# Loading the first weights of a mixer kernel in joint quarters of Wq and Wk, ahead of the transposing DMA

## The chip, the cores and the metric

The kernel runs on one core of one Trainium2 chip. TensorE (PE) multiplies matrices into PSUM, which has 8 banks of 128 x 512 float32; VectorE (DVE) and ScalarE (ACT) do the element-wise work, GpSimd (POOL) a few memsets, SyncE (SP) issues DMAs, and so can ACT. Each engine runs its own instructions in the order written and waits for others at semaphores. The metric is the device time of one execution in microseconds, as the median of several runs.

## The reference

One input x of 2048 rows (S) and 512 columns (D), in bfloat16, goes through two branches that a gate mixes:

```python
qkv = x @ wqkv                       # 512 -> 3 x 512, 32 heads of 16
# A: each position attends to 8 positions: itself and 2, 4, ... 14 back
logits = einsum(q, kg) * scale; attn = softmax(logits)
a = einsum(attn, vg) @ wo
# B: layernorm over D, then an MLP over the 2048 positions
u = gelu(w1.T @ layernorm(x) + b1)   # 1792 x 512
b = w2.T @ u + b2                    # 2048 x 512
g = sigmoid(sum(x * gate_w, -1))
out = g * a + (1 - g) * b
```

## The kernel before

Everything lives in one block of SBUF (`arena`). x is held twice: as rows (X, 16 tiles of 128 x 512, for layernorm and the MLP) and transposed (XT, four blocks of 128 columns of D by 2048 positions, for the projections). PE's work in order is:

1. seven warm-up matmuls on a constant (L536, written into bank 7), with four small ones (L544) between them that transpose a part of x,
2. the projections (L617) of Q and K, then V. An output group `dl` of 128 takes every fourth column of a weight, so four groups make 512, and each group has four matmuls, one for each quarter `dt` of the 512 rows of the weight; four blocks `sb` of 512 positions,
3. two bursts of 64 small matmuls (L696) that sum DVE's products of Q and shifted K (L688) over the head's 16 elements,
4. the MLP's first matmul (L810), its second (L860), and the attention's output projection (L876).

ACT evicts the projections from PSUM into Q5 (L625), K5 and V5 (L628); K5 has a pad of zeros in front, set by a POOL memset (L420). DVE computes the statistics of layernorm (L572), the products of Q and K (L688), softmax, the products with V (L795, L798), and at the end the mix (L897).

The order on each engine is found while the program is built. Each operation is given a duration, reads and writes, and a list scheduler (`_Sched`) places it at the earliest possible time; loads at the start have a landing time written by hand (`lands`), with the waits for earlier loads cleared. For DVE most of the order is written out by hand (`chain`): the statistics of tiles 0 to 3 come before the first product of Q and K, which reads Q and K of blocks 0 and 1. The bursts L696 have a high priority and go in where their products are planned to be ready. On the chip each engine keeps the planned order, whatever the real times.

The start concerns us. x's block 0 (positions 0 to 511) is transposed in two ways. Its columns 0 to 127 are loaded plainly by ACT's queue (`d_xp`, into XP), transposed by the four matmuls L544 and evicted by ACT (L553) and DVE (L555). Its columns 128 to 511 come by one transposing DMA on SP's queue (`ld_xt0`, L473, called xt0 here). Wq comes in four quarters of 128 KB: the first on ACT's queue behind the plain columns, the others on SP's behind xt0. Wk follows in two halves of 256 KB, then rows of x (`x0`: tiles 0 and 1), then the transposing DMA for block 1 (`xt1`, L460), x2, x4 (tiles 4 to 7), xt2, xt3 and the rest. L429 issues the plain DMAs.

PE's first projections (block 0) go over eight banks: Q's four groups in banks 0 to 3, K's four in banks 4 to 7. Banks 0 to 3 take quarter 0 in turn, then quarters 1, 2 and 3; then banks 4 to 7 take quarters 0 and 1, and then 2 and 3. From block 1 on, groups take all four quarters at once and rotate over banks 0 to 3, so each waits for the eviction of the group four before it:

```python
first = [(tn, dl) for tn in range(2) for dl in range(4)]
for (b0, d0, d1, s0, s1) in ((0, 0, 1, 0, 512), (0, 1, 2, 0, 512), (0, 2, 3, 0, 512),
                             (0, 3, 4, 0, 512), (4, 0, 2, 0, 512), (4, 2, 4, 0, 512)):
    for b in range(b0, b0 + 4):
```

Of the kernel before, what the change touches and what calls it, by code (L numbers as in the profile page):

```python
# [13 lines left out]
D = 512  # L14
# [6 lines left out]
PAD = 14  # L21
SC = 512
KROW = S + 32
# [310 lines left out]
def bass_gated_mix__sliding_local_dilated__mixer_token_mlp__prompt_kernel(nc, A_x, A_wqkv, A_wo, B_x, B_w1, B_b1, B_w2, B_b2, gate_w, out, dbg=None):  # L334
    with contextlib.ExitStack() as es:
# [3 lines left out]
        sch = _Sched()  # L339
# [3 lines left out]
        wqkv_v = A_wqkv.rearrange("(dt p) c -> p dt c", p=128)  # L343
# [7 lines left out]
        WQKV = view("WQKV", BF16, [(3 * D, 4), (1, 3 * D)])  # L351
# [10 lines left out]
        K5 = view("K5", BF16, [(KROW, 4), (1, KROW)])  # L362
# [45 lines left out]
        def sub(ap_, offs, dims):  # L408
            return bass.AP(ap_.tensor, ap_.offset + offs, [list(ap_.ap[0])] + [list(d) for d in dims])

        def psub(ap_, p0, np_, offs, dims):
# [3 lines left out]
        A = sch.add  # L415
# [1 line left out]
        c_ident = A("pool", lambda e: e.affine_select(out=IDENT, in_=nc.const_aps.tensor(1.0, [128, 128], BF16), pattern=[[1, 128]], compare_op=ALU.is_equal,  # L417
                                                     fill=0.0, base=0, channel_multiplier=-1),
                    0.4, writes=["ident"], name="ident")
        A("pool", lambda e: e.memset(sub(K5, 0, [(KROW, 4), (1, PAD)]), 0.0), 0.2, writes=["k5pad"], name="k5pad")  # L420
        A("pool", lambda e: e.memset(sub(V5, 0, [(KROW, 4), (1, PAD)]), 0.0), 0.2, writes=["v5pad"], name="v5pad")
        def f_rp(e):
            with nc.allow_low_precision(reason="exact 0/1 indicator sums"):
# [4 lines left out]
        def mk_dma(dst, src):  # L428
            return lambda e: e.dma_start(dst, src)  # L429

        init_dmas = []

        def throttle():
            return [init_dmas[-5]] if len(init_dmas) >= 5 else []

        def prev_dma():
            return [init_dmas[-1]] if init_dmas else []

        def ld_x(t0, n, q="sp"):
            ds = sch.dsem("x%d" % t0)  # L440
            op = sch.dma(q, mk_dma(X[:, t0:t0 + n, :], xv[:, t0:t0 + n, :]), n * 128 * D * 2, ds,
                         writes=["x%d" % t for t in range(t0, t0 + n)], deps=throttle() if q == "sp" else [], after=prev_dma() if q == "sp" else [], name="d_x%d" % t0)
            if q == "sp":
                init_dmas.append(op)
            return op

        def ld_w(tn, d0, n, q="sp"):
            ds = sch.dsem("wqkv%d_%d" % (tn, d0))
            op = sch.dma(q, mk_dma(WQKV[:, d0:d0 + n, tn * D:(tn + 1) * D], wqkv_v[:, d0:d0 + n, tn * D:(tn + 1) * D]),
                         n * 128 * D * 2, ds, writes=["wqkv%d_%d" % (tn, dt) for dt in range(d0, d0 + n)],  # L450
                         deps=throttle() if q == "sp" and n == 4 else [], after=prev_dma() if q == "sp" else [],
                         issue=0.65 if n == 4 else 0.45, name="d_wp%d_%d" % (tn, d0))
            if q == "sp":
                init_dmas.append(op)
            return op

        def ld_xt(sb):
            ds = sch.dsem("xt%d" % sb)
            dst = XT[:, :, sb * 512:(sb + 1) * 512]
            op = sch.dma("sp", lambda e: e.dma_start_transpose(dst, x2d[sb * 512:(sb + 1) * 512, :]), 512 * D * 2, ds,  # L460
                         writes=["xt_%d" % t for t in range(4 * sb, 4 * sb + 4)], deps=throttle(), after=prev_dma(), name="d_xt%d" % sb)
            init_dmas.append(op)
# [4 lines left out]
        def xt_of(sb, d0=0, d1=4):  # L467
            return XT0[d0:d1] + (XT0[4:] if d0 == 0 else []) if sb == 0 else ["xt_%d" % t for t in range(4 * sb, 4 * sb + 4)]

        def ld_xt0():  # L470
            ds = sch.dsem("xt0")
            dst = XT[:, 1:4, 0:512]
            op = sch.dma("sp", lambda e: e.dma_start_transpose(dst, x2d[0:512, 128:512]), 512 * 384 * 2, ds, issue=1.25,  # L473
                         writes=XT0[1:4], after=prev_dma(), name="d_xt0")
            init_dmas.append(op)
            return op

        XP = view("OUTS", BF16, [(128, 4), (1, 128)])
        d_xp = sch.dma("act", mk_dma(XP, xv[:, 0:4, 0:128]), 512 * 128 * 2, sch.dsem("xp"), writes=["outs0"], issue=0.4, name="d_xp")

        first_loads = [ld_w(0, 0, 1, "act"), ld_xt0(), ld_w(0, 1, 1), ld_w(0, 2, 1), ld_w(0, 3, 1), ld_w(1, 0, 2), ld_w(1, 2, 2),
                       ld_x(0, 2)]
        ld_xt(1)
        first_loads.append(init_dmas[-1])
        for op_, t_ in zip(first_loads, (3.4, 4.6, 5.0, 5.4, 5.8, 6.6, 7.4, 8.2, 10.6)):
            op_.lands = t_
            op_.deps.clear()
        d_xp.lands = 3.1
        first_loads[0].order.add(d_xp)
        init_dmas[:] = [first_loads[1]] + first_loads[5:]  # L490
        ld_x(2, 2)
        ld_x(4, 4)
        ld_xt(2)
# [6 lines left out]
        def ld_w1(j):  # L500
# [4 lines left out]
            if j < 4:  # L505
# [8 lines left out]
                       writes=["wo"], deps=throttle(), after=prev_dma(), name="d_wo")  # L514
# [4 lines left out]
        for i_, (v_, n_) in enumerate(((B_b1, NFT), (B_b2, NST))):  # L519
            vr = v_.rearrange("(t q j) -> q t j", q=4, j=32)  # L520
            for q_ in range(4):
                sch.dma("sp", mk_dma(psub(BR, 32 * q_, n_, 32 * i_, [(1, 32)]), vr[q_]), n_ * 64, ds_b, reads=["br"],
                        writes=["br_%d_%d" % (i_, q_)], deps=throttle(), after=prev_dma(), name="d_b_%d_%d" % (i_, q_), issue=0.45)
        d_w1.append(ld_w1(3))
        A("dve", lambda e: e.transpose(out=BT, in_=BR), 0.2, reads=["br_%d_%d" % (i_, q_) for i_ in range(2) for q_ in range(4)],
          writes=["btc"], name="t_b")
# [5 lines left out]
        def f_warm(n, w_=D):  # L532
            def fn(e):
                ins = None
                for _ in range(n):
                    ins = e.matmul(ps[:, 7, 0:w_], lhsT=CONE[:, 0:128], rhs=CONE[:, 0:w_], start=True, stop=True)  # L536
                return ins
            return fn

        def f_tr(h):  # L540
            def fn(e):
                ins = None
                for t in range(2):
                    ins = e.matmul(ps[:, 5 + h, 128 * t:128 * t + 128], lhsT=XP[:, 2 * h + t, :], rhs=IDENT, start=True, stop=True)  # L544
                return ins
            return fn
# [2 lines left out]
        w2_ = A("pe", f_warm(1, 256), 0.2, writes=["lg7_0", "lg7_1"], name="warm2", prio=-100)  # L549
        ta_ = A("pe", f_tr(0), 0.215, reads=["outs0", "ident"], writes=["lg5_0", "lg5_1"], after=[w2_], name="tr0", prio=-100)  # L550
        tr_ = A("pe", f_tr(1), 0.215, reads=["outs0", "ident"], writes=["lg6_0", "lg6_1"], after=[ta_], name="tr1", prio=-100)
        w3_ = A("pe", f_warm(1), 0.43, writes=["lg7_0", "lg7_1"], after=[tr_], name="warm3", prio=-100)
        A("act", lambda e: e.activation(out=XT[:, 0, 0:256], in_=ps[:, 5, 0:256], func=AF.Copy), 0.35, reads=["lg5_0", "lg5_1"],  # L553
          writes=["xt0_0"], name="ev_tra", prio=0)
        A("dve", lambda e: e.tensor_copy(out=XT[:, 0, 256:512], in_=ps[:, 6, 0:256]), 0.35, reads=["lg6_0", "lg6_1"],  # L555
          writes=["xt0_0b"], name="ev_trb", prio=0)
# [55 lines left out]
        def f_proj(tn, dl, sb, bank, d0=0, d1=4, s0=0, s1=512):  # L612
            def fn(e):
                ins = None
                for dt in range(d0, d1):
                    lhsT = sub(WQKV, dt * 3 * D + tn * D + dl, [(4, 128)])
                    ins = e.matmul(ps[:, bank, s0:s1], lhsT=lhsT, rhs=XT[:, dt, sb * 512 + s0:sb * 512 + s1],  # L617
                                   start=(dt == 0 and s0 == 0), stop=(dt == 3))
                return ins
            return fn  # L620
# [9 lines left out]
        tnames = ["q", "k", "v"]  # L630
        first = [(tn, dl) for tn in range(2) for dl in range(4)]
        fbn = [["acc%d" % b] for b in range(4)] + [["lg%d_0" % b, "lg%d_1" % b] for b in range(4, 8)]
        for (b0, d0, d1, s0, s1) in ((0, 0, 1, 0, 512), (0, 1, 2, 0, 512), (0, 2, 3, 0, 512), (0, 3, 4, 0, 512), (4, 0, 2, 0, 512), (4, 2, 4, 0, 512)):
            for b in range(b0, b0 + 4):
                tn, dl = first[b]
                last_main[0] = A("pe", f_proj(tn, dl, 0, b, d0, d1, s0, s1), 0.216 * (d1 - d0) * (s1 - s0) / 512,
                                 reads=xt_of(0, d0, d1) + ["wqkv%d_%d" % (tn, dt) for dt in range(d0, d1)],
                                 writes=fbn[b], after=[last_main[0]], name="pf_%s%d_%d_%d" % (tnames[tn], dl, d0, s0))
                last_main[0].order.add(w3_)
        for b, (tn, dl) in enumerate(first):  # L640
            A("act", f_evq(tn, dl, 0, b), 0.52, reads=fbn[b] + (["k5pad"] if tn == 1 else []),
              writes=["%s5_%d_0" % (tnames[tn], dl)], name="ev_%s%d_0" % (tnames[tn], dl), prio=0)
# [7 lines left out]
        for (tn, dl, sb) in seq_proj:  # L650
# [4 lines left out]
                             writes=["acc%d" % bank], after=[last_main[0]], name="pj_%s%d_%d" % (tnames[tn], dl, sb), prio=0)  # L655
            A("act", f_evq(tn, dl, sb, bank), 0.62, reads=["acc%d" % bank] + (["k5pad"] if tn == 1 else ["v5pad"] if tn == 2 else []),
              writes=["%s5_%d_%d" % (tnames[tn], dl, sb)], name="ev_%s%d_%d" % (tnames[tn], dl, sb), prio=0)
# [11 lines left out]
                writes=["xa"] + ["wqkv%d_%d" % (tn, dt) for tn in range(3) for dt in range(4)], name="d_xa")  # L669
        for t in range(NST):  # L670
# [5 lines left out]
          writes=["th"], name="g_tanh", prio=0)  # L676
# [31 lines left out]
        for wh in range(2):  # L708
# [6 lines left out]
            for (dl, c0, nc_) in pieces:  # L715
# [5 lines left out]
                  writes=wr, name="qkm_%d_%d_%d" % (wh, dl, c0), prio=0)  # L721
            rd = sum([pbn(b_) for b_ in bufs], []) + PBX[wh] + ["rp"]
            for wl in range(4):
                qop = A("pe", f_qkr(list(enumerate(bufs)), (wl,)), 0.92, reads=rd, writes=["lg%d_0" % (4 + wl), "lg%d_1" % (4 + wl)],
                        name="qkr_%d_%d" % (wh, wl), prio=-100 + wl, delay=BURST_DELAY)
                A("act", (lambda wh_, wl_: (lambda e: e.activation(out=ATT[:, :, 4 * wh_ + wl_, :], in_=ps[:, 4 + wl_, :].rearrange("p (h c) -> p h c", h=2), func=AF.Copy)))(wh, wl),  # L726
                  0.55, reads=["lg%d_0" % (4 + wl), "lg%d_1" % (4 + wl)], writes=["lw%d" % (4 * wh + wl)],
                  name="lev_%d_%d" % (wh, wl), prio=0)
# [60 lines left out]
        for k_, u in enumerate(USEQ):  # L789
# [7 lines left out]
            for (nm, n_, du) in (("ava", 4, 2.25), ("avb", 2, 1.2)):  # L797
                A("dve", (lambda pv_, n__: (lambda e: e.tensor_tensor(out=pv_[:, 0:n__], in0=pv_[:, 0:n__], in1=pv_[:, n__:2 * n__], op=ALU.add)))(pv, n_),  # L798
                  du, writes=[pn], name="%s_%d" % (nm, u))
# [27 lines left out]
        for ft in range(NFT):  # L827
# [6 lines left out]
              name="gel_%d" % ft, prio=0)  # L834
# [84 lines left out]
        for i in range(NST):  # L919
# [4 lines left out]
            elif i > 1:  # L924
# [6 lines left out]
              name="t1_%d" % i, prio=0)  # L931
# [119 lines left out]
```

## Time and profile before

| what | value |
|---|---|
| median of 3 runs | 168.18 us (167.72 to 168.53) |
| the profiled execution's own time | 168.55 us |
| its span | 167.3 us |
| granted PE clock | 1.00 |
| first projection matmul (L617) starts | 5.61 us |
| first product of Q and K (L688) starts | 15.07 us |
| last combine (L897) ends | 165.65 us |

The span goes from the first to the last instruction of one profiled execution; times of single instructions count from its start. The page gives busy time by engine, the chain of work that ended last, and groups of instructions by line of the kernel; further answers of the trace give waits, single stretches of time, and for each DMA the time from its issue to its landing. A line such as `arena<-in_A_x_dram` reads "written tile <- read tensor". "SPq" and "ACTq" are the queues on which SP and ACT issue DMAs.

### The profile page before, as it was taken

Reading aid. Unit: us, or ns where it says so; the run is one execution under the profiler, and the core shown is the slowest. Engines: PE = TensorE matmul, PEld = TensorE weight load, DVE = VectorE, ACT = ScalarE, POOL = GpSimd, SP = SyncE. Lnnn points to the kernel's source line nnn. Section 1 sums busy time; section 2 is a strip of 40 time slices with the busy share of each in tenths; the row PEclk is TensorE's granted clock in tenths of the full one; section 3 lists DMA queues with packets and bytes.
Section 4 is the critical chain, followed back from the end, with each engine's and each line's share of the span. In section 5 each row is a group of like instructions: output and inputs, shape, how many; then the busy total and the mean of one; then the engine's idle time right before and its main releaser. Section 6 shows DMA issues by size and latency. Waiting matters only on the chain.

```text
span 167.3 us, 2136 instructions
## 1 busy us (share of the span) xinstructions
PE 162.1 (97%) x845; PEld 77.5 (46%) x859; DVE 151.3 (90%) x154; ACT 75.1 (45%) x116; POOL 0.7 (0%) x8
## 2 busy tenths in 40 slices
PE   7699999999999999999999999999999999999994
PEld 2355555554454444444444444444444444444463
DVE  1055999999999999999999999999999999999896
ACT  3077688889899818793131121131231321310100
POOL 1000000000000000000000000000000000000000
PEclk9999999999999999999999999999999999999999
DMA  5999999959003846996779926462672570000454
GB/s 135 327 268 216 314 316 290 303 165 308 2 0 97 311 116 179 307 290 155 181 189 340 339 76 142 113 187 71 181 218 83 138 223 0 0 0 0 157 190 159
DMA packets 47625, 29.64 MB, mean 177 GB/s; under 512 B 9856, under 2 KB 46464, under 8 KB 47616
## 3 DMA queue, kind: packets, MB, share of 16 engines
q1 hardware_dynamic: 45120, 24.85, 54.4%
q10 hardware_dynamic: 2496, 4.66, 10.2%
q8 instruction: 7, 0.11, 0.3%
q14 instruction: 2, 0.02, 0.0%
HBM read 21.24 MB, written 2.10 MB: 140 GB/s over the span
## 4 chain that ended last, share of the span: by engine, by line
PE 91%; DMA 3%; DVE 2%; ACT 2%; issue 1%; ACTq 0%
PE ps L860 29%; PE ps L810 29%; PE ps L617 23%; PE ps L876 6%; PE ps L696 4%; DMA arena<-in_A_wqkv_dram 3%; DVE arena L897 2%; ACT L585 1%; ACT arena L628 1%; ACTq L429 0%; ACT arena L585 0%
## 5 line engine op out<-in xcount | busy, mean ns | idle before, releaser
L860 PE MATMUL ps<-arena 128*128 128x512 bf16 x220 | 48.5, 379 | 0.2
L810 PE MATMUL ps<-arena 128*128 128x512 bf16 x219 | 48.2, 379 | 0.4 <-issue 0.2
L617 PE MATMUL ps<-arena 128*128 128x512 bf16 x188 | 41.4, 379 | 1.6 <-DMA arena<-in_A_wqkv_dram 1.3
L688 DVE TENSOR_TENSOR arena<-arena 128x4096 bf16<-128x4096 bf16 (+1 forms) x12 | 35.5, 2998 | 2.5 <-ACT arena L628 2.1
L795 DVE TENSOR_TENSOR arena<-arena 128x8192 bf16<-128x8192 bf16 x8 | 35.0, 4419 | 0.0
L860 PEld LDWEIGHTS ps<-arena 128*128 128x128 bf16 x224 | 21.9, 98 | 26.4
L810 PEld LDWEIGHTS ps<-arena 128*128 128x128 bf16 x224 | 21.8, 98 | 26.6 <-ACT arena L726 0.4
L617 PEld LDWEIGHTS ps<-arena 128*128 128x128 bf16 x192 | 21.6, 113 | 21.5 <-issue 1.8
L928 ACT ACTIVATE arena<-ps,arena 128x512 bf16<-128x512 f32 x16 | 12.5, 778 | 39.4 <-PE ps L860 39.4
L798 DVE TENSOR_TENSOR arena<-arena 128x4096 bf16<-128x4096 bf16 (+1 forms) x16 | 27.0, 1751 | 0.0
L628 ACT ACTIVATE arena<-ps 128x512 bf16<-128x512 f32 x32 | 18.6, 596 | 4.5 <-PE ps L617 4.5
L831 ACT ACTIVATE arena<-ps,arena 128x512 bf16<-128x512 f32 x14 | 9.6, 687 | 22.2 <-PE ps L810 16.6
L572 DVE BATCH_NORM_STATS2 arena<-arena 128x6 f32<-128x512 bf16 x16 | 10.0, 682 | 6.1 <-DMA arena<-in_A_x_dram 6.1
L876 PE MATMUL ps<-arena 128*128 128x512 bf16 (+1 forms) x79 | 14.1, 336 | 0.1
L897 DVE SCALAR_TENSOR_TENSOR arena<-ps,arena 128x512 bf16<-128x512 f32 (+1 forms) x20 | 11.5, 637 | 0.9 <-PE ps L876 0.7
L596 ACT ACTIVATE arena<-arena 128x512 bf16<-128x512 bf16 x16 | 12.2, 804 | 0.0
L625 ACT ACTIVATE arena<-ps 128x512 bf16<-128x512 f32 x16 | 9.0, 597 | 6.2 <-PE ps L617 6.1
L876 PEld LDWEIGHTS ps<-arena 128*128 128x128 bf16 x80 | 7.8, 98 | 6.2
L672 DVE SCALAR_TENSOR_TENSOR arena<-arena 128x512 bf16<-128x512 bf16 x16 | 10.1, 689 | 0.0
L742 DVE TENSOR_TENSOR arena<-arena 128x512 bf16<-128x512 bf16 (+4 forms) x11 | 7.3, 667 | 0.6 <-ACT arena L761 0.2
L696 PE MATMUL ps<-arena 128*32 128x512 bf16 x128 | 7.3, 380 | 0.0
L726 ACT ACTIVATE arena<-ps 128x512 bf16<-128x512 f32 x8 | 4.7, 592 | 4.6 <-PE ps L696 4.6
(42 smaller groups left out, 40.0 us busy)
## 6 DMA issues: line engine op xcount, KB each, us to landing
arena<-in_B_w_dram SPq DMA_DIRECT2D x7, 1024.0 KB, 8.5
arena<-in_B_w_dram SPq DMA_DIRECT2D x8, 896.0 KB, 5.2
arena<-arena ACTq DMA_DIRECT2D x32, 128.0 KB, 2.9
arena<-in_A_x_dram SPq DMA_DIRECT2D x4, 512.0 KB, 6.1
out_dram<-arena SPq DMA_DIRECT2D x14, 128.0 KB, 1.7
arena<-in_A_x_dram SPq DMA_DIRECT2D x1, 1536.0 KB, 7.9
arena<-in_A_wqkv_dram SPq DMA_DIRECT2D x2, 256.0 KB, 3.8
arena<-in_A_x_dram SPq DMA_DIRECT2D x2, 256.0 KB, 3.6
```

The costliest lines, as they stand in the source:

```text
L596: A("act", (lambda t_: (lambda e: e.activation(out=X[:, t_, :], in_=X[:, t_, :], func=AF.Identity, scale=col(RSTD, t_), bias=col(NMR, t_)) ...
L617: ins = e.matmul(ps[:, bank, s0:s1], lhsT=lhsT, rhs=XT[:, dt, sb * 512 + s0:sb * 512 + s1], start=(dt == 0 and s0 == 0), stop=(dt == 3))
L628: return lambda e: e.activation(out=dst, in_=ps[:, bank, :], func=AF.Copy)
L688: return lambda e: e.tensor_tensor(out=PBL[buf][:, :, 512 * c0:512 * (c0 + nc_)], in0=in0, in1=in1, op=ALU.mult)
L696: ins = e.matmul(ps[32 * c:32 * c + 32, 4 + wl, :], lhsT=RP, rhs=PBL[buf][:, wl, c * 512:(c + 1) * 512], start=(dl == 0), stop=(dl == 3), ...
L795: A("dve", (lambda o_, i0, i1: (lambda e: e.tensor_tensor(out=o_, in0=i0, in1=i1, op=ALU.mult)))(pv, in0, in1), 4.4, reads=v_res + ["atx_% ...
L798: A("dve", (lambda pv_, n__: (lambda e: e.tensor_tensor(out=pv_[:, 0:n__], in0=pv_[:, 0:n__], in1=pv_[:, n__:2 * n__], op=ALU.add)))(pv, n ...
L810: ins = e.matmul(ps[:, bank, :], lhsT=W1W[:, slot, st, 128 * e_:128 * e_ + 128], rhs=X[:, st, :], start=(st == 0), stop=(st == NST - 1))
L860: ins = e.matmul(ps[:, bank, :], lhsT=W2S[slot][:, ft, 128 * e_:128 * e_ + 128], rhs=UT[:, ft, :], start=(ft == 0), stop=(ft == NFT - 1))
L876: ins = e.matmul(ps[:, bank, 0:c1 - c0], lhsT=OT[:, t, 128 * i:128 * i + 128], rhs=WO[:, t, c0:c1], start=(t == 0), stop=(t == 3))
L897: A("dve", (lambda i_, b_, c0_, c1_: (lambda e: e.scalar_tensor_tensor(out=T1[:, i_, c0_:c1_], in0=ps[:, b_, 0:c1_ - c0_], scalar=col(G, i ...
L928: A("act", (lambda i_, bank_: (lambda e: e.activation(out=T1[:, i_, :], in_=ps[:, bank_, :], func=AF.Identity, scale=col(OMG, i_), bias=co ...
```

## The change

The first quarter of Wq and the first quarter of Wk are loaded by one DMA of 256 KB (their columns lie side by side in the weight, so a row gives 2 KB), and so are the second, third and fourth quarters. All four go on SP's queue: the first ahead of xt0, the others behind it. ACT's queue is left with the plain columns. The first joint quarter waits for POOL's memset of K5's pad, which has nothing to do with its data; by this wait it is issued later than the plain columns. The transposing DMA of block 1 is now issued ahead of the first rows of x. Planned landings are rewritten. The warm-up gets one more matmul of 256 columns. PE's first projections take quarter 0 over all eight banks, then quarter 1 over all eight, then banks 0 to 3 take quarter 2 and quarter 3, and banks 4 to 7 take both in one go.

```diff
-        A("pool", lambda e: e.memset(sub(K5, 0, [(KROW, 4), (1, PAD)]), 0.0), 0.2, writes=["k5pad"], name="k5pad")
+        c_kp = A("pool", lambda e: e.memset(sub(K5, 0, [(KROW, 4), (1, PAD)]), 0.0), 0.2, writes=["k5pad"], name="k5pad")
...
-        first_loads = [ld_w(0, 0, 1, "act"), ld_xt0(), ld_w(0, 1, 1), ld_w(0, 2, 1), ld_w(0, 3, 1), ld_w(1, 0, 2), ld_w(1, 2, 2),
-                       ld_x(0, 2)]
+        def ld_qk(d):
+            ds = sch.dsem("wqk%d" % d)
+            op = sch.dma("sp", mk_dma(WQKV[:, d, 0:2 * D], wqkv_v[:, d, 0:2 * D]), 2 * 128 * D * 2, ds,
+                         writes=["wqkv0_%d" % d, "wqkv1_%d" % d], after=prev_dma(), issue=0.45, name="d_wqk%d" % d)
+            init_dmas.append(op)
+            return op
+
+        first_loads = [ld_qk(0), ld_xt0(), ld_qk(1), ld_qk(2), ld_qk(3)]
         ld_xt(1)
         first_loads.append(init_dmas[-1])
-        for op_, t_ in zip(first_loads, (3.4, 4.6, 5.0, 5.4, 5.8, 6.6, 7.4, 8.2, 10.6)):
+        first_loads.append(ld_x(0, 2))
+        for op_, t_ in zip(first_loads, (4.0, 5.2, 6.0, 6.7, 7.4, 9.6, 10.4)):
             op_.lands = t_
             op_.deps.clear()
         d_xp.lands = 3.1
-        first_loads[0].order.add(d_xp)
-        init_dmas[:] = [first_loads[1]] + first_loads[5:]
+        first_loads[0].deps.add(c_kp)
+        init_dmas[:] = [first_loads[1]] + first_loads[3:]
...
-        w3_ = A("pe", f_warm(1), 0.43, writes=["lg7_0", "lg7_1"], after=[tr_], name="warm3", prio=-100)
+        A("pe", f_warm(1), 0.43, writes=["lg7_0", "lg7_1"], after=[tr_], name="warm3", prio=-100)
+        w3_ = A("pe", f_warm(1, 256), 0.2, writes=["lg7_0", "lg7_1"], after=[tr_], name="warm4", prio=-100)
...
-        for (b0, d0, d1, s0, s1) in ((0, 0, 1, 0, 512), (0, 1, 2, 0, 512), (0, 2, 3, 0, 512), (0, 3, 4, 0, 512), (4, 0, 2, 0, 512), (4, 2, 4, 0, 512)):
-            for b in range(b0, b0 + 4):
+        for (b0, nb, d0, d1, s0, s1) in ((0, 8, 0, 1, 0, 512), (0, 8, 1, 2, 0, 512), (0, 4, 2, 3, 0, 512), (0, 4, 3, 4, 0, 512),
+                                         (4, 4, 2, 4, 0, 512)):
+            for b in range(b0, b0 + nb):
```

## The prediction

> **What bounds the kernel now.** First the page's busy shares, then the chain that ended last, then who waited for whom on PE and DVE.
>
> ```profile
> PE 162.1 (97%) x845; PEld 77.5 (46%) x859; DVE 151.3 (90%) x154; ACT 75.1 (45%) x116; POOL 0.7 (0%) x8
> ```
>
> ```profile
> 0.80 0.46 ACTq L429
> 1.25 0.03 issue
> 1.28 4.24 DMA arena<-in_A_wqkv_dram
> 5.52 0.09 issue
> 5.61 8.36 PE ps L617 x38
> ...
> 161.67 3.98 DVE arena L897 x9
> ```
>
> ```profile
> PE ps L617 <- DMA arena<-in_A_wqkv_dram: 1.3, 1, 1.3
> ...
> PE ps L617 <- ACT arena L585: 0.2, 1, 0.2
> ```
>
> ```profile
> DVE arena L688 <- ACT arena L628: 2.1, 1, 2.1
> DVE arena L688 <- PE ps L696: 0.4, 1, 0.4
> ...
> DVE arena L897 <- PE ps L876: 0.7, 1, 0.7
> ```
>
> PE is the chain. Its one sizeable wait behind the warm-up is 1.3 us, ended at 5.52 by the quarter of Wq that ACT issued at 1.28; from 5.61 on it hardly stops. DVE is close behind: from its first long product (15.07) to the end it stands still for about 1.3 us in all. So the change is worth what it moves PE's first stage, if DVE follows.
>
> The first loads, each from the DMA answers for its own moment (last number: us from issue to landing), and the transposing issues from the timeline:
>
> ```profile
> arena<-in_A_wqkv_dram ACTq DMA_DIRECT2D x1, 128.0 KB, 4.2
> arena<-in_A_x_dram SPq DMA_TRANSPOSE x1, 4.9
> ```
>
> ```profile
> 0.80 1.35 SPq L473 DMA_TRANSPOSE arena<-in_A_x_dram  x1
> ...
> 5.27 3.36 SPq L460 DMA_TRANSPOSE arena<-in_A_x_dram  x1
> ...
> 9.81 3.77 SPq L460 DMA_TRANSPOSE arena<-in_A_x_dram  x1
> ```
>
> Landings so worked out: plain columns 3.2, Wq0 5.5, xt0 5.7, Wq1 6.0 (issued 2.22), Wq2 6.2, Wq3 6.6, Wk's halves 7.5 and 8.2, x0 8.85, xt1 10.8, x2 11.7 (issued 8.67). Wq0, with 128 KB, took longer than any other of its size and landed just ahead of xt0.
>
> **The clock of the sum.** Matmuls of the first stage go at 0.217 us: the first eviction (8.62) ends 13 of them begun at 5.61. The 33rd starts at 5.61 + 32 x 0.217 = 12.55. After the change the first eight need only the first joint quarter and the plain columns; from the ninth on PE needs xt0 and the second joint quarter. If that ninth starts at D, the 33rd starts at D + 24 x 0.217 = D + 5.21. So the gain is 7.34 - D: break-even at 7.34.
>
> **The first joint quarter** (256 KB). SP waits for the memset of K5's pad (POOL, 1.12 + 0.14), so it issues near 1.30. To landing: the plain columns, 128 KB on empty queues, took 2.4; another 128 KB at the 0.29 MB/us moved there add 0.45: 2.85. Bounds are 2.4 and the 3.7 of Wk's first half in a backlog. I take 2.85, nearest in conditions: landed at 4.15 (3.7 to 5.0). Queued behind SP's wait are all loads of SP. PE's start is then bounded by the warm-up: the last tile of transposed columns is evicted at 4.38, the added 256-column warm-up matmul (half of the 0.43 pitch of slow ones) frees PE near 4.56. I take 4.6; eight matmuls end at 6.35.
>
> **xt0 behind it.** Its issue no longer starts at 0.80 but near 1.85. Three transposing issues in this trace end 0.2 us ahead of the landing of the DMA in front of them on SP's queue (8.63 against x0's 8.85, 13.58 against x4's 13.8, 15.63 against xt2's 15.8), however early they begin; xt0, with nothing in front, took 1.35. So its issue would end near 3.95, not 3.2. From there the 512 KB ones land 2.1, 2.2 and 2.7 later, the 384 KB of xt0 itself 3.55 later, beside the plain columns and Wq0, which no longer lie beside it. I take 1.9: 5.85 (5.55 to 7.5).
>
> **The second joint quarter**, issued near 4.0. Rows: x2, 256 KB right behind a 512 KB transpose, 3.0; Wq1, right behind xt0, 3.8. Less 128 KB in front, x2's row gives 2.55. I take 2.8, between and nearer x2's, which has the same size: 6.8 (6.55 to 7.8). With 0.09 from landing to matmul, **D = 6.9**, gain 0.44. PE's wait of 1.3 becomes one of about 0.3 ahead of the first eight and one of 0.55 ahead of the ninth.
>
> **The third and fourth** follow at the 0.7 to 0.9 between Wk's halves and x0: 7.6 and 8.4; needed at D + 1.74 = 8.65 and D + 2.6 = 9.5. Hidden, cover about 1 us.
>
> **SP's issues.** Three of 0.43 and two of some 0.45 go, four of some 0.5 come, and xt0's issue may be stretched by 0.75. xt1 begins near 5.5 (before 5.27), ends by the same rule near 8.2 and lands by 10.9; needed at 12.1. x0 goes behind it: issued 8.25 instead of 4.75, landed near 11.3 instead of 8.85; x2 near 12.1. The four statistics (0.69 first, then 0.6 each) end near 13.9 instead of 13.0; DVE's first product needs them by 14.85, cover about 0.95. If that is gone, DVE loses what is missing. Transposes 2 and 3 had 3 us to spare.
>
> **ACT.** The issue of Wq0 (0.53) goes; ACT had waited there for PE anyway, so nothing. But bank 0 is finished 20 matmuls after the first eight's start in place of 12: its eviction starts at D + 3.0 = 9.9 (before 8.62), and the eight first evictions then run back to back at the 0.48 seen between them. The tenth, which starts DVE's first product, starts at 9.9 + 9 x 0.48 = 14.2 where PE would allow 14.05. DVE starts at 14.85 in place of 15.07: it gains 0.2 where PE gains 0.44. The planner books 0.52 for each, so it may put the next burst of score matmuls (L696) one projection (0.87) later; DVE, which waits 0.4 there, would then be 0.87 - 0.44 = 0.43 late. The tail has 0.7 to 0.9 of DVE idle ahead of the last combines, so about 0.4 still reaches the end.
>
> **The sum.** The profiled execution has a span of 167.3 and a time of 168.55, so 1.25 lies around the span. 167.3 - 0.4 = 166.9 gives 168.15 by that execution; it stands 0.37 above the median. Against the median: 168.18 - 0.4 = **167.8**. By the bounds of the second quarter (6.55 to 7.8) and a floor at 6.35, the gain lies between 1.0 and a loss of 0.55.
>
> **Rivals.** 0.5% (0.84 us) is about what a measurement of this kernel can tell from no change.
>
> *Faster: nothing holds xt0 back.* If the stretched issues of the three later transposes come from the depth of backlog (up to six loads) and not from the load just in front, xt0's issue ends at 3.2 and everything moves up: the second quarter lands about 6.0 to 6.6, D is 6.35 to 6.7, the time 167.2 to 167.55. For it: xt0 had a short issue; DMA carried about 300 GB/s from 2 us on, and the bytes up to the second quarter are those that had landed at 6.6 before. Against: three of three end at the landing in front.
> [...]
>
> *Slower: xt0's own time.* If the 3.55 from the end of its issue to landing belongs to this transfer and not to its neighbours, it lands at 3.95 + 3.55 = 7.5; with a first quarter landing at 4.5 rather than 4.15, 7.85, and the second quarter 0.3 behind, as Wq1 was behind xt0: D near 8.2, gain -0.86, time 169.05. It decides from D = 7.34. For it: it is the only row of this very transfer, and Wq1's 3.8. Against: the 512 KB transposes did it in 2.1 to 2.7.
>
> *The slow clock reaches into the first eight.* Warm-up matmuls stood 0.43 apart and lasted 631 ns up to 4.34; at 5.61 they lasted 379. Where between them the speed changed, no row shows. The change starts the real ones 1 us earlier: all eight at 0.43 end at 4.6 + 3.4 = 8.0, D = 8.0, time 168.85. Half of them slow end at 7.2, 0.3 behind my D.
> [...] The granted clock in the profile's rows reads 1.00 throughout and doesn't show it; the two durations agree that there is a switch.
>
> *The gain is given back on DVE.* If the planner moves the burst by two projections, DVE is 1.75 - 0.44 = 1.3 late, and past the 0.9 of the tail 0.4 to 0.5 remain: 168.65; more if both bursts move or x2 lands after 13.1. For it: DVE has no idle from 15.07 but 1.3. Against: its first wait is PE's burst, which moves with PE.
>
> **How the numbers follow.** Forecast (D from 6.7 to 7.6, 167.55 to 168.45): 0.42. Nothing holds xt0: 0.18. xt0's own time: 0.20. Slow clock: 0.06. DVE: 0.14. Faster than 167.34 are 13 in 100 from the second case and 5 from the forecast's edge: 0.18. Slower than 169.02: 15 of xt0's own time, 7 of DVE, 2 of the clock: 0.24. The rest, 0.58, is no change. The range goes from 167.1, just beyond the floor of 6.35, to 169.1, just beyond xt0's own time; about 0.15 is left out, most of it above.
>
> **What would show it.** In the changed trace: the first quarter issued at 1.3 and landed near 4.15; the first L617 matmul near 4.6 in place of 5.61; xt0's issue lasting about 2.1, ending 0.2 ahead of the first quarter's landing; a wait of PE for a weight load of some 0.55 with matmuls again at 6.9; the first eviction near 9.9 and L628 back to back with it; DVE's first L688 near 14.85; the burst at 38.1, or one projection later. I am wrong if the ninth matmul starts after 7.6 (xt0 or the second quarter), if the first eight lie 0.43 apart, or if PE gains and the last L897 does not move.

## The result: slower, and the profile after

The changed kernel takes 170.73 us in the median (170.1 to 171.19, 4 executions) against 168.11 of the kernel before (167.72 to 168.53): the ratio is 1.015, with a 95% interval from 1.012 to 1.018. Forecast were 167.8 and a range up to 169.1, so the time lies outside and on the other side. Of 45 later executions of the kernel before, 33 took 167.7 to 168.7 us and 12 took 169.6 to 170.9, and the ratios below count some of the longer ones, which can make a variant look up to 0.2% better than beside the 33. The profiled execution of the changed kernel has a span of 169.0 (before 167.3) and a time of 170.37 (before 168.55).

The start of the chain that ended last, changed kernel (start, length, what):

```profile
0.80 3.73 DMA arena<-in_A_x_dram
4.53 0.14 issue
4.66 0.58 PE ps L551 x4
5.25 0.64 PE ps L543 x2
5.89 9.61 PE ps L625 x37
...
163.41 3.98 DVE arena L906 x9
```

In place of the quarter of Wq that ACT issued, the plain columns of x stand at the head. They landed at 4.53; before, issued in the same moment, at 3.2. The waits of PE and the waits of DVE say the same:

```profile
PE ps L551 <- DMA arena<-in_A_x_dram: 1.3, 1, 1.3
PE ps L543 <- PEq L1045: 0.8, 1, 0.8
PE ps L625 <- ACT arena L593: 0.2, 1, 0.2
```

```profile
DVE arena L697 <- ACT arena L636: 3.4, 1, 3.4
```

The wait for a weight load ahead of the first projections is gone, as forecast. The same 1.3 us now stand ahead of the transposing matmuls, inside the warm-up, where before there was none. The timeline around SP's first load shows why:

```profile
0.80 0.46 ACTq L429 DMA_DIRECT2D arena<-in_A_x_dram  x1
0.80 0.14 POOL L420 MEMSET arena<- 128x56 bf16 x1 [0.29 <-POOLq L1045]
...
0.96 0.29 POOL L417 TENSOR_SCALAR_AFFINE_SELECT arena<-const-bfloat16-1.0 128x128 bf16<-128x128 bf16 x1
0.97 0.39 SPq L429 DMA_DIRECT2D arena<-in_A_wqkv_dram  x1
```

POOL now clears K5's pad (L420) ahead of building the identity (L417); before it was the other way round. The first load of SP waits for the pad, so the planner took the memset for urgent and put it first. The joint quarter went out at 0.97, only 0.17 us behind the columns, and not at 1.3.

The second loss is in the weight loads of the first projections (the column PEld), each of which goes with one matmul:

```profile
5.76 0.15 PEld L625 LDWEIGHTS ps<-arena 128*128 128x128 bf16 x2 [0.57 <-DVE arena L563]
6.18 0.15 PEld L625 LDWEIGHTS ps<-arena 128*128 128x128 bf16 x1 [0.27 <-issue]
6.61 0.15 PEld L625 LDWEIGHTS ps<-arena 128*128 128x128 bf16 x1 [0.28 <-issue]
...
8.74 0.15 PEld L625 LDWEIGHTS ps<-arena 128*128 128x128 bf16 x1 [0.28 <-issue]
9.08 0.11 PEld L625 LDWEIGHTS ps<-arena 128*128 128x128 bf16 x1 [0.19 <-issue]
```

All first eight projections stand 0.43 apart, and only at 9.08 does PE go to 0.217. Before, none of the first projections was slow. So the span divides as follows: the first projection starts 0.16 later (5.77 against 5.61), and eight of them take 9.08 - 5.76 = 3.32 in place of 1.74, which is 1.58 more. Together that is 1.74, and the last stretch of DVE begins 163.41 - 161.67 = 1.74 later. DVE's first product of Q and K shows the same step, first before, then after the change:

```profile
15.07 2.29 DVE L688 TENSOR_TENSOR arena<-arena 128x4096 bf16<-128x4096 bf16 x1 [2.06 <-ACT arena L628]
16.82 2.29 DVE L697 TENSOR_TENSOR arena<-arena 128x4096 bf16<-128x4096 bf16 x1 [3.43 <-ACT arena L636]
```

From its start to that last stretch it is 146.6 us in each of nine profiles (after, after_again, before, before_again, before_fill1, filled_gap, pool_order, pool_order_fill1 and split_second). So nothing behind the first stage adds or takes away, and a run's time can be read from where this product starts.

The medians differ by 2.62. Of this, 1.82 lie between the two profiled executions; 0.44 come from the profiled execution of before having stood above its median, and 0.36 from that of the changed kernel having stood below its own. The experiments take up the three parts: the late columns, the slow matmuls, and what kind of execution the profile of before had shown.

### The profile page after: what moved, and what is told of

Same layout as the page of the kernel before. It is cut to its first block, busy times and chain, and to the rows that moved or that the text cites. A ratio compares the mean times of both kernels' runs of the same rounds, so it can differ in the third digit from the quotient of the medians.

```text
span 169.0 us, 2135 instructions
## 1 busy us (share of the span) xinstructions
PE 163.7 (97%) x846; PEld 77.9 (46%) x860; DVE 151.2 (89%) x154; ACT 74.8 (44%) x116; POOL 0.8 (0%) x8
## 4 chain that ended last, share of the span: by engine, by line
PE 93%; DVE 2%; DMA 2%; issue 1%
PE ps L869 28%; PE ps L819 28%; PE ps L625 25%; PE ps L885 6%; PE ps L705 4%; DVE arena L906 2%; DMA arena<-in_A_x_dram 2%; PE ps L543 0%; PE ps L551 0%
## 5 line engine op out<-in xcount | busy, mean ns | idle before, releaser
L869 PE MATMUL ps<-arena 128*128 128x512 bf16 x220 | 48.5, 379 | 0.2
L819 PE MATMUL ps<-arena 128*128 128x512 bf16 x219 | 48.2, 379 | 0.4 <-issue 0.2
L625 PE MATMUL ps<-arena 128*128 128x512 bf16 x188 | 43.0, 389 | 0.3 <-ACT arena L593 0.2
L636 ACT ACTIVATE arena<-ps 128x512 bf16<-128x512 f32 x32 | 18.8, 600 | 3.5 <-PE ps L625 3.4
L633 ACT ACTIVATE arena<-ps 128x512 bf16<-128x512 f32 x16 | 9.3, 602 | 8.2 <-PE ps L625 8.2
L735 ACT ACTIVATE arena<-ps 128x512 bf16<-128x512 f32 x8 | 4.7, 592 | 4.6 <-PE ps L705 4.6
```

What stands on the lines that cost most here:

```text
L636: return lambda e: e.activation(out=dst, in_=ps[:, bank, :], func=AF.Copy)
L819: ins = e.matmul(ps[:, bank, :], lhsT=W1W[:, slot, st, 128 * e_:128 * e_ + 128], rhs=X[:, st, :], start=(st == 0), stop=(st == NST - 1))
L869: ins = e.matmul(ps[:, bank, :], lhsT=W2S[slot][:, ft, 128 * e_:128 * e_ + 128], rhs=UT[:, ft, :], start=(ft == 0), stop=(ft == NFT - 1))
```

## The experiments

### Only the order on POOL undone

```diff
-        c_kp = A("pool", lambda e: e.memset(sub(K5, 0, [(KROW, 4), (1, PAD)]), 0.0), 0.2, writes=["k5pad"], name="k5pad")
+        c_kp = A("pool", lambda e: e.memset(sub(K5, 0, [(KROW, 4), (1, PAD)]), 0.0), 0.2, writes=["k5pad"], name="k5pad", after=[c_ident])
```

> The changed kernel with one thing undone: on POOL the identity is built ahead of K5's pad again, as before the change, so that the first joint quarter is issued near 1.3 us instead of 0.97. Theory (the joint quarter takes the DMA engines from the plain columns, which then land at 4.53 instead of 3.2; PE stands idle in its warm-up from 3.35 to 4.66 and its clock stays slow over the first eight projections): the plain columns land by 3.5, the transposing matmuls start by 3.6, the first projections are fast (pitch 0.217) or slow for two of them at most, the ninth starts near 6.9, and the time is 167.5 to 168.2. Rival (the slow matmuls come from the phase of the clock's switch, not from the gap): slow matmuls up to about 9 us all the same, 169.5 to 170.7. Second rival (the columns are late because of xt0 or of the size of the joint quarter, whenever it is issued): columns at 4.3 or later, time above 169.5.

168.75 us in the median (168.29 to 169.3, 10 executions), ratio to before 1.0021 (0.9984 to 1.0057). The joint quarter goes out at 1.29, and the DMA answer for this moment gives for the columns and the quarter:

```profile
arena<-in_A_wqkv_dram SPq DMA_DIRECT2D x1, 256.0 KB, 3.0
arena<-in_A_x_dram ACTq DMA_DIRECT2D x1, 128.0 KB, 2.3
```

Issued 0.32 us later, the quarter lands near 4.3, as in the changed kernel; the columns land at 3.1 in place of 4.53. PE's timeline:

```profile
4.36 1.92 PE L625 MATMUL ps<-arena 128*128 128x512 bf16 x8 [0.19 <-DVE arena L563]
7.08 0.38 PE L625 MATMUL ps<-arena 128*128 128x512 bf16 x1 [0.81 <-DMA arena<-in_A_wqkv_dram]
```

The first eight start at 4.36 and are fast; the ninth starts at 7.08. Nothing else in the program's order differs from the changed kernel, so both late columns and slow matmuls come from this one exchange on POOL. Both rivals fall. DVE's first product starts at 14.82 (forecast 14.85; 15.07 in the profile of before), so this execution, the fastest of its ten, has about the gain that was forecast beside that profile. Still, the time was at most expected at 168.2, and the median of 168.75 is no faster than before. The second profile of the kernel before and the spread of the second joint quarter, both below, say why.

### The gap in the warm-up filled

```diff
-        A("pe", f_warm(5), 2.13, writes=["lg7_0", "lg7_1"], name="warm1", prio=-100)
+        A("pe", f_warm(8), 3.41, writes=["lg7_0", "lg7_1"], name="warm1", prio=-100)
```

> The changed kernel with eight warm-up matmuls in front instead of five, so that PE is busy until about 4.5 us; the plain columns stay as late as they are (4.5). Theory (the gap in the warm-up keeps the clock slow): first projections start near 5.8, at a pitch of 0.217, the ninth near 7.5, the 33rd near 12.7 (12.55 before the change): time 168.1 to 168.6. Rival (phase of the switch): slow until about 9 us as in the changed kernel, 170.0 to 171.2.

168.75 us (168.41 to 169.1, 10 executions), ratio 1.003 (1.000 to 1.006). The columns take 3.7 as in the changed kernel, and PE's transposing matmuls start at 4.63. Yet the weight loads of the first projections now merge into one row:

```profile
5.73 3.38 PEld L625 LDWEIGHTS ps<-arena 128*128 128x128 bf16 x17 [0.57 <-DVE arena L563]
```

17 loads in 3.4 us: all at 0.2. Three matmuls whose results nobody reads take 2.0 us off the changed kernel's 170.73. So the late columns alone cost little (0.4 in the profiles: DVE's first product at 15.22, against 14.82 with the order on POOL undone); the rest of what they cost lies in the slow matmuls. The miss of 0.15 above the expected range is left open.

### The same gap put into the kernel before

```diff
-        A("pe", f_warm(5), 2.13, writes=["lg7_0", "lg7_1"], name="warm1", prio=-100)
+        A("pe", f_warm(2), 0.85, writes=["lg7_0", "lg7_1"], name="warm1", prio=-100)
```

> The kernel before with two warm-up matmuls in front instead of five: PE stands idle from about 2.1 to 3.3 us, the loads are untouched. Theory: the first projections, which start at 5.61 as before, are slow for some 2 to 3.4 us, so 1.0 to 1.7 us are lost: 169.1 to 169.9. Rival (phase): no change, 168.1.

169.42 us (169.01 to 170.93, 4 executions), ratio 1.010 (1.004 to 1.016). PE waits 1.2 for the columns in its warm-up, and then:

```profile
4.61 0.14 PEld L617 LDWEIGHTS ps<-arena 128*128 128x128 bf16 x2 [0.89 <-DVE arena L555]
5.02 0.15 PEld L617 LDWEIGHTS ps<-arena 128*128 128x128 bf16 x1 [0.27 <-issue]
...
7.16 0.15 PEld L617 LDWEIGHTS ps<-arena 128*128 128x128 bf16 x1 [0.28 <-issue]
7.56 0.55 PEld L617 LDWEIGHTS ps<-arena 128*128 128x128 bf16 x3 [0.25 <-issue]
```

Seven slow projections without any of the change's loads. Filling the gap in one kernel and opening it in the other move the time in opposite directions, and pool_order, with the changed kernel's matmuls and no gap, starts fast: the gap is shown as the cause of the slow start. The first projection started at 4.61, though, and not at 5.61 as expected: the first quarter of Wq had landed at 4.55.

Where PE worked without a gap from 0.84 on, its first fast matmul came at 3.9 (the last of the warm-up in pool_order) to 6.0 (first_on_ident, below), 3.1 to 5.2 us later. An idle time of 0.8 to 1.3 us, ahead of the first fast matmul, moved it to 7.56 here and to between 9.08 and 9.76 in the four profiles with late columns and an unfilled gap. In these five PE had by then worked again for 4.3 to 5.3 us, close to the upper part of the 3.1 to 5.2 without a gap; what sets the moment, no run shows. Idle time is not harmful everywhere. In the first profile of the kernel before, PE stood still for as long right behind 3.5 us of warm-up, and the projections after it were fast:

```profile
3.71 0.63 PE L536 MATMUL ps<-const-bfloat16-1.0 128*128 128x512 bf16 x1
5.61 10.74 PE L617 MATMUL ps<-arena 128*128 128x512 bf16 x48 [1.26 <-DMA arena<-in_A_wqkv_dram]
```

The granted clock in the rows stayed at 1.00 throughout; only pitch (0.43 against 0.217 us) and duration (631 against 379 ns) tell slow matmuls from fast ones. That a clock makes the difference was the author's assumption and was not shown.

### A second profile of either kernel

> The kernel before, unchanged, profiled a second time. Question: is the late first quarter of Wq (landed at 5.52, first projection at 5.61) what this kernel does, or what one execution did? If it is the rule: 5.3 or later again. If it varies, as the run with the gap suggests (4.55): landing between 4.3 and 5.3, the first projection right behind it, and no wait of 1.3 us left for the change to remove.

> The changed kernel, unchanged, profiled a second time. Theory (slow clock through the gap that the late plain columns leave): columns at 4.3 to 4.7, gap of about 1.3 in the warm-up, first projections at a pitch of 0.43 for 6 to 12 matmuls, span 168.7 to 170.0. If the first run's slow clock was chance: fast projections, span 167.3 or less.

The kernel before: span 166.8, time 168.21. The first quarter of Wq, issued at 1.28, took 3.2 and landed at 4.5. The waits of PE:

```profile
PE ps L617 <- DMA arena<-in_A_wqkv_dram: 0.6, 2, 0.4
```

and the first projections in its timeline:

```profile
4.61 3.73 PE L617 MATMUL ps<-arena 128*128 128x512 bf16 x16 [0.37 <-DMA arena<-in_A_wqkv_dram]
```

So the wait of 1.3, from which the prediction took the whole gain, is not there in every execution. Over four profiles with these loads the quarter landed at 5.52, 4.5, 4.55 and 5.4 (the last in a run below): twice late, twice early. And the earlier start was worth less than it looks: 1.0 us earlier at the first projection, 0.44 at DVE's first product (14.63 against 15.07), 0.5 in the span. Wk's first half, 7.5 in the first profile, landed at 8.52 in this one, and PE waited for it: the first stage is paced by several loads, not by the first alone.

The changed kernel: span 169.3, time 170.52; columns 3.5 from issue to landing, 1.1 of waiting in the warm-up, and ten slow projections from 5.58 on, the last at 9.41:

```profile
9.41 0.15 PEld L625 LDWEIGHTS ps<-arena 128*128 128x128 bf16 x1 [0.28 <-issue]
9.76 0.33 PEld L625 LDWEIGHTS ps<-arena 128*128 128x128 bf16 x2 [0.21 <-issue]
```

Its slow start was no chance.

### The second joint quarter split

```diff
-        first_loads = [ld_qk(0), ld_xt0(), ld_qk(1), ld_qk(2), ld_qk(3)]
+        first_loads = [ld_qk(0), ld_xt0(), ld_w(0, 1, 1), ld_w(1, 1, 1), ld_qk(2), ld_qk(3)]
...
-        for (b0, nb, d0, d1, s0, s1) in ((0, 8, 0, 1, 0, 512), (0, 8, 1, 2, 0, 512), (0, 4, 2, 3, 0, 512), (0, 4, 3, 4, 0, 512),
+        for (b0, nb, d0, d1, s0, s1) in ((0, 8, 0, 1, 0, 512), (0, 4, 1, 2, 0, 512), (4, 4, 1, 2, 0, 512), (0, 4, 2, 3, 0, 512), (0, 4, 3, 4, 0, 512),
```

The order on POOL is undone as above, and the list of planned landings gets one more entry; the order of the matmuls stays.

> As the run with the order on POOL undone, but the second joint quarter split into a quarter of Wq and one of Wk, of 128 KB each, on the same queue, with Q's four matmuls of that quarter ahead of K's in the same order. Theory (the size of the second joint quarter sets the ninth matmul, 7.05 there): the ninth starts at 6.4 to 6.7 and the time falls by 0.3 to 0.5 against that run, to about 168.3. Rival (xt0 and the time from issue to landing set it, whatever the size): the ninth at 6.9 or later, no gain, 168.7.

168.1 us (167.57 to 168.87, 10 executions), ratio 1.0001 (0.9979 to 1.0024). The second quarter of Wq, issued at 3.31, took 2.9 and landed at 6.2, that of Wk near 7.0; the joint one, issued at 3.63, had come at 6.95, and Q's matmuls need only the first. PE no longer waits:

```profile
4.34 3.06 PE L625 MATMUL ps<-arena 128*128 128x512 bf16 x12
```

Twelve without a stop (the first two slow). The ninth starts at 6.37, and the profiled execution has the shortest span of the study, 166.3. Of the 0.7 by which the load lands earlier, 0.4 is its shorter way and 0.3 its earlier issue, which the split doesn't explain. Still, 128 KB in this place took 2.9 here, the joint 256 KB 3.2 to 4.3 in six profiles (3.3 and 4.2 in the changed kernel, 3.3 in pool_order, 3.2 in filled_gap, 4.1 in pool_order_fill1, 4.3 in first_on_ident). So the size is confirmed in the trace as part of what held the ninth matmul, and the rival falls. DVE's first product comes at 14.11 and no longer waits for ACT:

```profile
14.11 2.29 DVE L697 TENSOR_TENSOR arena<-arena 128x4096 bf16<-128x4096 bf16 x1
```

But the statistics of tiles 0 to 3, which stand ahead of it in DVE's order, end only at 14.10, because the rows of x land later in the new order (x0 at 11.6, before 8.9). In this execution a still earlier ninth matmul would gain nothing without earlier rows. In time the split's worth is less clear: the median is 0.65 below that of the run without it, but of the ratios to the kernel before, each taken beside it, the second is only 0.2%, 0.3 us, lower (by the medians 0.5 us), and the two intervals overlap. Against the kernel before the measurement finds no difference: even with its own wait in PE's first stage gone, the new order of loads buys nothing that can be measured. Why the ten executions spread over 1.3 us, and most lie above the profiled one, no profile of them shows.

### One more warm-up matmul

```diff
-        A("pe", f_warm(5), 2.13, writes=["lg7_0", "lg7_1"], name="warm1", prio=-100)
+        A("pe", f_warm(6), 2.56, writes=["lg7_0", "lg7_1"], name="warm1", prio=-100)
```

> As the run with the order on POOL undone, with six warm-up matmuls in front instead of five, so PE is busy without a gap from 0.84 to its first projections if the columns land by 3.6. Theory: within 0.4 us of that run, 167.5 to 168.2, with no slow projections or two at most. Rival (phase): as that run, with slow projections, above 169.5.

> The kernel before with six warm-up matmuls in front instead of five, nothing else. Theory (slow clock by a gap in the warm-up is what makes its scattered longer times, up to 170.9): the transposing matmuls start 0.2 later, the first projection is set by the weight as before, median 168.1 to 168.4 and no time above 169.3. Rival (the longer times have another cause): the same scatter up to 170 and more.

With the order on POOL undone: 168.79 us (168.44 to 169.28), ratio 1.0035 (1.0006 to 1.0064), no slow projections, and the same as without the matmul within their spread; it lies above the range expected. The second joint quarter took 4.1 from issue to landing in this execution (3.3 in the other), and the ninth matmul started at 7.57. In the kernel before: 168.26 us (167.67 to 170.32), ratio 0.9988 (0.9959 to 1.0017). One of ten executions took 170.32, against the expectation that none would exceed 169.3. So what lengthens single executions of the kernel before stays open. This run neither supports nor excludes a gap as its cause: one in ten is not clearly fewer than 12 in 45, and PE still stands idle for 0.9 ahead of its first projection. None of the 40 executions of pool_order, filled_gap, pool_order_fill1 and split_second, where PE is idle for at most 0.2 at that place, took more than 169.3. The author's guess is that in some executions PE turns fast only after the idle time of the kernel before has begun: that began at 4.34 in the first profile, and without a gap the first fast matmul came at 3.9 to 6.0. But none of its long executions was profiled.

### How far behind the columns the first load must stay

Three variants of the changed kernel, one execution profiled of each. In the first, the first joint quarter has no wait (the line with `c_kp` is gone); in the second it waits for the identity; in the third it waits for the pad as in the changed kernel, but only Wq's part of it, 128 KB, goes ahead (the list of planned landings again gets one more entry).

```diff
-        first_loads[0].deps.add(c_kp)
+        first_loads[0].deps.add(c_ident)
...
-        first_loads = [ld_qk(0), ld_xt0(), ld_qk(1), ld_qk(2), ld_qk(3)]
+        first_loads = [ld_w(0, 0, 1), ld_xt0(), ld_w(1, 0, 1), ld_qk(1), ld_qk(2), ld_qk(3)]
```

> The changed kernel without the wait of the first joint quarter, which SP then issues at 0.80, in the same moment as ACT the plain columns. Theory (whatever joint quarter is issued less than some 0.3 us behind the columns delays them): columns land at 4.5 or later (4.53 in the changed kernel at 0.97, 3.1 with the order on POOL undone at 1.29), slow first projections, above 169.5. Rival (the delay at 0.97 is not an effect of the distance): columns by 3.5.

> The changed kernel with the first joint quarter waiting for the identity instead of the pad; POOL then builds the identity first, so the issue comes near 1.2 us, 0.1 ahead of the run with the order on POOL undone. If the delay grows evenly with the overlap, the columns land at 3.4 to 3.6 (4.53 at 0.97, 3.1 at 1.29); if it is all or nothing, by 3.2 or at 4.3.

> The changed kernel with only the first quarter of Wq (128 KB) ahead of xt0, issued at 0.97 as the joint quarter is; Wk's comes behind xt0. If the columns wait for all bytes of the load beside them, they land 0.45 earlier than in the changed kernel, near 4.1; if the number of its rows matters and not their length (128 rows of 1 KB instead of 2 KB), near 4.5 again; if they are only slowed by sharing, near 3.5.

| run | load beside the columns | issued at | columns land at |
|---|---|---|---|
| first_no_wait | 256 KB | 0.80 | 4.2 |
| after, after_again | 256 KB | 0.97 | 4.53, 4.3 |
| small_first | 128 KB | 0.97 | 4.0 |
| first_on_ident | 256 KB | 1.20 | 3.1 |
| pool_order | 256 KB | 1.29 | 3.1 |

The columns were issued at 0.80 each time. In these profiles it is a step, not a slope: at a distance of 0.40 us the columns lost nothing, at 0.17 some 1.2 to 1.4, although the change of distance is only 0.23, and at 0 they lost 1.1. That excludes an even growth with the overlap. With no wait at all they landed at 4.2, earlier than the 4.5 that was expected, but late all the same. Half the bytes beside them made 0.3 to 0.5 less delay than 256 KB issued in the same moment, near the expected 0.45 for a wait behind all bytes; the rivals by rows (4.5) and by mere sharing (3.5) fit worse, but it is one execution. Not every load beside the columns delayed them: in the kernel before, the 384 KB of xt0 were issued in the same moment, and they landed at 3.1 to 3.2. What in the load of weights does it is not shown. The times are of single executions, 170.22, 169.29 and 170.26, beside 170.25 for the one of the kernel before, and show nothing by themselves. In first_on_ident, without a gap, the first four projections were still slow. It shows the other weak point of the joint quarters, too:

```profile
4.35 2.68 PE L625 MATMUL ps<-arena 128*128 128x512 bf16 x8
8.00 0.38 PE L625 MATMUL ps<-arena 128*128 128x512 bf16 x1 [0.98 <-DMA arena<-in_A_wqkv_dram]
```

Here the second joint quarter took 4.3 from its issue at 3.58, and PE stood for 1.0 ahead of the ninth matmul. From 3.2 to 4.3 is what this load took in the six profiles named above; the prediction had 2.8.

## Why the prediction was wrong, step by step

**The step that failed** is "The first joint quarter": "SP waits for the memset of K5's pad (POOL, 1.12 + 0.14), so it issues near 1.30." The 1.12 was read from the trace of before, and with it POOL's order of before. Among operations that can start at the same time the planner takes the one with the most work hanging on it, and the change itself had hung the first load on this memset. It started at 0.80 and the load at 0.97. In the same step the bound of the warm-up ("evicted at 4.38") took the columns' landing of 3.2 as untouched. It measured 4.53, and the eviction ended at 5.71. A new load of 256 KB within 0.2 us of another's issue was priced for what it waits, not for what it takes from the other.

**The slow clock** was a rival with 0.06 and a price of 0.7. It was what happened, but by another mechanism than stated: not because the real matmuls came too early (they came at 5.77, later than before), but because the late columns opened a gap in the warm-up: 1.3 us, ahead of first projections that stood 0.43 apart until 9.08. filled_gap and before_gap show it from both sides. That the matmuls are slow by a clock, or when its switch comes, no run shows.

**The wait to be removed** was taken from one execution. The gain of 7.34 - D stood on a first projection at 5.61; a second profile had it at 4.61, with DVE's first product 0.44 earlier. The sum noted that the profiled execution stood 0.37 above the median, and yet took the gain over it from the median. The spread of the three times before, 0.8 us, could have been a hint. This, with the second joint quarter below, is, as far as the profiles show, why pool_order, whose ninth matmul starts at 7.08 in its profile (forecast 6.9), doesn't beat the kernel before.

**xt0 held back by the load in front** was wrong in its mechanism: its issue ended at 3.1, 3.6 and 3.2 (changed kernel, pool_order, pool_order_fill1), while the first quarter landed at 4.3, 4.3 and 4.2. The rival that nothing holds it back (3.2) was nearer. The rule does hold again for block 1 in the changed kernel: its issue ended at 4.71 + 3.21 = 7.92, and the load in front landed at 8.1. What tells the two apart was not tried. xt0's landing (5.6 to 5.8 in all nine profiles of the new order; forecast 5.85) came out nearly right all the same, by an earlier issue and a longer way from there, which is luck, and the rival "xt0's own time" (7.5) falls.

**The second joint quarter**: forecast 6.8, within 6.55 to 7.8. It landed at 6.5 and 7.8 in the two profiles of the changed kernel, 6.95, 7.4 and 7.9 in pool_order, pool_order_fill1 and first_on_ident. The range was about right, but by two errors that cancel, which is luck: it was issued at 3.15 to 3.65 instead of 4.0, and took 3.2 to 4.3 instead of 2.8. With 7.4 to 7.9 the ninth matmul comes at 7.57 to 8.0, past the break-even of 7.34. In the changed kernel itself it was not the bound, as the slow matmuls ended later.

**ACT's evictions** were right: the first one came 3.01 after the ninth matmul in pool_order (forecast D + 3.0), and DVE's first product 4.73 later (forecast 9 x 0.48 + 0.63 = 4.95). It followed the ninth eviction, though, not the tenth.

**DVE and the bursts**: the planner left them where they were; the bursts start 1.74 later, as everything does, and DVE's idle ahead of the last combines is 0.7 as before. That rival falls.

## What to carry to other kernels

A wait that is added to delay a load also makes what it waits for urgent, and a planner may move that forward (here POOL's memset, from 1.12 to 0.80); fix the order of both, or wait for something whose time is set by other means. Before a wait is priced as a gain, look at more than one execution: here the same load landed at 5.52 and at 4.5, and of the 1.0 us by which PE began earlier, 0.44 were left at DVE's first product, because the next load landed later (8.52 against 7.5). And keep warm-up work gapless until PE's matmuls have turned fast, here 3.1 to 5.2 us after its start: three matmuls that nobody reads were worth 2.0 us.

## What the runs showed that was not expected

- A 128 KB load of 256-byte pieces, issued first, landed 1.1 to 1.4 us later when a 256 KB load of rows of 2 KB was issued on the other queue in the same moment or 0.17 us behind it, and not later at all when that came 0.40 behind (4.2 to 4.53 against 3.1).
- The load that came in its way hardly profited from an issue at 0.97 in place of 1.29: it landed near 4.3 in the changed kernel and in pool_order. Issued at 0.80, it landed at 3.7.
- An idle gap of 0.8 to 1.3 us in the warm-up kept matmuls at a pitch of 0.43 until 7.6 to 9.8 us; without it they were fast by 3.9 to 6.0.
